# A clustered-attention, mixture-of-experts and gated feed-forward kernel: buffers of their own for the cluster sums' copy and the comparison's output

## The chip, the core and the metric

The kernel runs on one core of a Trainium2 chip. The metric is the device time of one execution in microseconds (us). The kernel before takes 869.03 us, the median of three runs that lie between 868.84 and 869.63 us.

## The reference

Three layers follow each other: attention in which a query sees only the keys of its own cluster, a layer of eight experts with one expert per token, and a gated feed-forward layer. Only the first is touched by the change. Cut to that:

```python
# q, k, v: (2, 8, 768, 64) f32; centroids: (8, 16, 64)
q_assign = argmax(einsum('bhsd,hcd->bhsc', q_n, c_n))   # nearest of 16 centroids, per head
k_assign = argmax(einsum('bhsd,hcd->bhsc', k_n, c_n))
mask   = q_assign[:, :, :, None] == k_assign[:, :, None, :]
scores = where(mask, q @ k.T / sqrt(64), -1e9)
attn   = softmax(scores)
x      = attn @ v                    # then the experts, then the gated layer
```

## The kernel before

Sixteen heads are worked through as eight pairs (`n` = 0 to 7). A pair has twelve steps `g`; in each step 128 queries of one head meet all 768 keys. TensorE makes the scores `s` (L338, two parts that are summed in PSUM: one from the tiles `Aq` and `Ak`, one from `qB` and `kB`), VectorE takes the negative row maximum `nm` (L341), ScalarE the exponential `P` (L351). TensorE turns `P` over (`t`, L367), ScalarE and VectorE copy the halves into `PT` (L370, L372), and after three steps TensorE multiplies with v (`acc`, L386). When both heads of a pair have finished a half of the queries, `onat` takes the reciprocal of the sums (`rs`, L411 and L412, VectorE), multiplies by `R` on TensorE (`on`, L416) and writes `lg` and `x` (L420, VectorE). This happens in steps 0 and 3 of the next pair.

Each engine works through its own instructions strictly in the order in which the program writes them (`manual_schedule`). Where an instruction waits, everything behind it on its engine waits too. The order inside a step is set by the list `order` in `CFG`: soft, scores, the two turns, the evacuation, one piece of preparation (B0), `onat` (O), the product with v (V0), further preparation (B1).

While pair n-1 is worked through, the next pair n is prepared in eight pieces, at the steps that `offs` gives, counted from the start of pair n-1:

- `q0` and `q1` at steps -4 and -2, `k0` and `k1` at -1 and 1 (`tr`): q and k are turned over in halves and split into a high part `Hq`, `Hk` and a low part `Lq`, `Lk` (the rounding error of the high part), and `X` is kept in full. With the second half, `moves` has SyncE issue the transfers that copy the parts into `Aq`, `Ak`, `qB`, `kB` of the pair: six for q and six for k, 192 KB each, among them `Aq<-Lq` and `kB<-Lk`, two each.
- `a` at step 2 (`assign`): the products with the centroids (`asp`), and ScalarE's copy of them into the tile `as` (L206).
- `t` at step 3 (`pick`): TensorE turns `as` over (`ast`, L213), VectorE takes the maximum per token (`mxa`, L218) and compares (`eqa`, L219), GpSimd multiplies the result by a descending count (L220).
- `f` at step 6 (`first`) picks the first maximum; `m` at step 7 (`mask`) turns the result over, ScalarE writes `oT` (L295), and SyncE issues eight small transfers `qB<-oT` and `kB<-oT` that append it to the operands of the scores.

Piece `t` stands at token B0 of step 3, and the later `onat` of the pair before follows it at token O. So VectorE's order there is `mxa`, `eqa`, `rs`, its reciprocal, `lg`, `x`.

Buffers come from pools. The pool `one` has a single buffer for each tag; two tiles with one tag share that buffer, and the writer of the second then waits for every reader of the first. In the kernel before, `as` has the tag `Lq` and `eqa` the tag `Lk`. The readers of `Lq` and `Lk` are the transfers `Aq<-Lq` and `kB<-Lk`. Pair 1 keeps its low parts in another pool (`raw`), pair 0 its own in `one`.

SyncE's queue carries, beside these moves, the loads of q, k and v of coming pairs (`load`) and eight fills of 768 KB with zeros (`moe_rows<-zero`, L594, one in every four steps from step 14 on).

Of the kernel before, what the change touches and what calls it, by code (L numbers as in the profile page):

```python
# [10 lines left out]
F32 = mybir.dt.float32  # L11
# [12 lines left out]
class Attention:  # L24
# [169 lines left out]
    def assign(self, n):  # L194

        nc, st = self.nc, self.pairs[n]
        C, HS = self.C, self.S // 2
        b, hp = divmod(n, self.H // 2)
        ps = self.ps_m.tile([128, HS], F32, tag="mm", name="asp")
        for half in range(2):  # L200
            for si, nm in enumerate("qk"):
                g = (2 * half + si) * 2 * C
                nc.tensor.matmul(ps[g:g + 2 * C], lhsT=self.cbd[:, hp, :], rhs=st["X" + nm][:, half * HS:(half + 1) * HS],
                                 start=True, stop=True, tile_position=(0, g))
        st["as"] = self.one.tile([128, HS], F32, tag="Lq", name="as")
        nc.scalar.copy(out=st["as"], in_=ps)  # L206

    def pick(self, n):
        nc, st = self.nc, self.pairs[n]
        C, HJ = self.C, self.J // 2  # L210
        ps = self.ps_m.tile([128, HJ, 128], F32, tag="mm", name="ast")
        for jj in range(HJ):
            nc.tensor.transpose(ps[:, jj, :], st["as"][:, jj * 128:(jj + 1) * 128], self.ident)  # L213
        G = HJ * 8
        psf = ps.rearrange("p j (g c) -> p (j g) c", c=C)
        mx = self.one.tile([128, G], F32, name="mxa")
        eq = self.one.tile([128, G, C], F32, tag="Lk", name="eqa")
        nc.vector.tensor_reduce(out=mx, in_=psf, axis=AX.X, op=ALU.max)  # L218
        nc.vector.tensor_tensor(out=eq, in0=psf, in1=mx.unsqueeze(2).to_broadcast([128, G, C]), op=ALU.is_equal)  # L219
        nc.gpsimd.tensor_tensor(out=eq, in0=eq, in1=self.desc.to_broadcast([128, G, C]), op=ALU.mult)  # L220
        st["eq"] = eq
# [980 lines left out]
```

## Time and profile before

| | |
|---|---|
| median of three runs | 869.03 us |
| the profiled execution's own time | 871.81 us |
| its span (first to last instruction) | 870.1 us |
| mean granted TensorE clock | 0.967 of full speed |
| attention up to pair 0's last scores | 0 to about 52 us |
| pairs 1 to 6 | about 52 to 306 us |
| pair 7 | about 306 to 342 us |
| experts and gated layer | 342 to 870 us |

The span of the profiled execution is 1.7 us shorter than its own time, and that time is 2.8 us above the median. Instructions are named by line, engine and tile, with the written tile to the left of the arrow. The clock column of the stretches is the share of full speed that TensorE was granted: 1.00 is 2.4 GHz, 0.50 is 1.2 GHz, and what lies between is a mixture of the two.

### The profile page before, as it was taken

What the parts mean: (1) busy time and instruction counts of PE and PEld (TensorE: products, weight loads), DVE (VectorE), ACT (ScalarE), POOL (GpSimd) and SP (SyncE); (2) the same over time, 40 slices, a digit from 0 to 9 for tenths busy, and PEclk for the clock granted to TensorE, in tenths of its full rate; (3) what the DMA queues carried; (4) which work ended last, traced back from release to release, by engine and by line L of the source; (5) the groups of instructions that cost most, each with busy time, mean ns of one, the idle gap of its engine ahead of it and who ended that gap; (6) DMA issues with size and microseconds to landing.
All of it is one profiled execution on the core that took longest, in us unless ns stands there. A gap on an engine that the chain in (4) does not pass through costs nothing. (4 is left out here: it accounts for less than half of the span.)

```text
span 870.1 us, 12695 instructions
## 1 busy us (share of the span) xinstructions
PE 796.2 (92%) x4791; PEld 661.3 (76%) x4791; DVE 530.9 (61%) x871; ACT 381.0 (44%) x697; POOL 191.8 (22%) x212
## 2 busy tenths in 40 slices
PE   8988787878697999899999999999999999999997
PEld 7755555556465667799999999887888888888885
DVE  5665555555556677676666565367776676676533
ACT  5664545454545565355545554245432232232110
POOL 5110101010102002640000000033433333333235
PEclk9998989798998999999999999999999999999999
DMA  9762737370705221766666666032321221220012
GB/s 199 177 146 99 174 107 176 106 168 9 165 10 139 70 86 61 266 206 206 205 194 197 200 203 194 25 97 82 112 72 52 73 71 51 73 73 0 1 49 97
DMA packets 94210, 102.04 MB, mean 117 GB/s; under 512 B 30752, under 2 KB 78752, under 8 KB 94144
## 3 DMA queue, kind: packets, MB, share of 16 engines
q1 hardware_dynamic: 89280, 89.33, 36.8%
q0 software_dynamic: 1920, 6.29, 1.9%
q10 hardware_dynamic: 2944, 5.54, 1.8%
q8 instruction: 41, 0.67, 0.3%
q14 instruction: 25, 0.20, 0.1%
HBM read 68.21 MB, written 12.58 MB: 93 GB/s over the span
## 5 line engine op out<-in xcount | busy, mean ns | idle before, releaser
L341 DVE TENSOR_REDUCE nm<-s 128x1 f32<-128x768 f32 x96 | 91.4, 952 | 77.8 <-PE s L338 77.1
L370 ACT COPY PT<-t 128x384 f32<-128x384 f32 x96 | 46.3, 482 | 129.5 <-PE t L367 128.9
L351 ACT ACTIVATE P<-s,nm 128x768 f32<-128x768 f32 x96 | 87.0, 907 | 9.2 <-DVE nm L341 5.9
L367 PE MATMUL t<-ident,P 128*128 128x128 f32 x576 | 81.5, 276 | 0.9 <-ACT PT L370 0.5
L386 PE MATMUL acc<-PT,ldv 128*64 128x384 f32 x384 | 77.1, 538 | 0.2 <-DVE rm L634 0.2
L1027 POOL TENSOR_TENSOR W1l<-cm,W1h 128x512 fp32r<-128x512 f32 x18 | 23.4, 1301 | 235.0 <-ACT W1h L1026 235.0
L367 PEld LDWEIGHTS t<-ident,P 128*128 128x128 f32 x576 | 69.1, 142 | 7.4 <-DVE PT L372 1.2
L844 PE MATMUL yp<-Hhh,W2h 128*128 128x256 f32 x256 | 73.2, 286 | 0.0
L844 PE MATMUL hp<-Xh,W1h 128*128 128x256 f32 x256 | 72.8, 284 | 0.2 <-ACT Xh L836 0.2
L844 PE MATMUL hp<-Xl,W1h 128*128 128x256 f32 x256 | 72.7, 284 | 0.3 <-DVE Xl L837 0.3
L844 PE MATMUL yp<-Hhh,W2l 128*128 128x256 f32 x256 | 72.6, 284 | 0.0
L844 PE MATMUL yp<-Hhl,W2h 128*128 128x256 f32 x256 | 72.5, 283 | 0.0
L844 PE MATMUL hp<-Xh,W1l 128*128 128x256 f32 x256 | 72.5, 283 | 0.0
L1054 POOL TENSOR_TENSOR ghl<-u,ghh 128x512 fp32r<-128x512 f32 x36 | 49.9, 1387 | 75.1 <-ACT ghh L1053 75.1
L338 PE MATMUL s<-Ak,Aq 128*128 128x384 f32 x192 | 59.5, 392 | 6.0 <-ACT P L351 6.0
L1073 DVE TENSOR_TENSOR acc<-o,acc 128x512 f32<-128x512 f32 x60 | 41.2, 691 | 31.0 <-PE o L1065 31.0
L416 PE MATMUL on<-R,O 128*128 128x144 f32 x96 | 19.9, 357 | 43.3 <-DVE rs L411 42.9
L1051 DVE TENSOR_TENSOR u<-sg,g 128x512 f32<-128x512 f32 x36 | 24.8, 688 | 54.3 <-ACT sg L1050 53.1
L338 PE MATMUL s<-kB,qB 80*128 80x384 f32 (+1 forms) x192 | 52.3, 348 | 4.8 <-DMA kB<-oT 4.0
L338 PEld LDWEIGHTS s<-Ak,Aq 128*128 128x128 f32 x192 | 29.6, 194 | 33.1 <-ACT P L351 22.8
L372 DVE COPY PT<-t 128x384 f32<-128x384 f32 x96 | 52.4, 546 | 1.5 <-PE t L367 1.5
L386 PEld LDWEIGHTS acc<-PT,ldv 128*64 128x64 f32 x384 | 27.2, 150 | 33.9 <-issue 31.8
(269 smaller groups left out, 2007.7 us busy)
## 6 DMA issues: line engine op xcount, KB each, us to landing
raw<-in_moe_w SPq DMA_DIRECT2D x64, 512.0 KB, 4.3
Ak<-Hk SPq DMA_DIRECT2D x32, 192.0 KB, 5.0
moe_rows<-zero SPq DMA_DIRECT2D x8, 768.0 KB, 6.0
raw<-in_moe_w_gate SPq DMA_DIRECT2D x12, 512.0 KB, 3.6
raw<-in_moe_w_val SPq DMA_DIRECT2D x12, 512.0 KB, 3.6
raw<-in_moe_w_out SPq DMA_DIRECT2D x12, 512.0 KB, 3.5
xr<-moe_rows ACTq DMA_DIRECT2D x7, 768.0 KB, 6.5
ldq<-in_q SPq DMA_DIRECT2D x16, 192.0 KB, 4.3
```

The costliest lines, as they stand in the source:

```text
L338: nc.tensor.matmul(ps[:, c, 0:HS], lhsT=ql[:, qs], rhs=kr[:, c * HS:(c + 1) * HS], start=a == 0, stop=a == 1)
L341: nc.vector.tensor_reduce(out=nm, in_=ps[:, :, 0:HS], axis=AX.XY, op=ALU.max, negate=True)
L351: nc.scalar.activation(out=P, in_=ps[:, :, 0:HS], func=AF.Exp, bias=nm, accum_out=self.pairs[n]["sum"][:, i, r:r + 1])
L367: nc.tensor.transpose(ps[:, jj, :], P[:, a, jj * 128:(jj + 1) * 128], self.ident)
L370: nc.scalar.copy(out=PT[:, js, cs], in_=ps)
L372: nc.vector.tensor_copy(PT[:, js, cs], ps)
L386: nc.tensor.matmul(acc[c * D:(c + 1) * D], lhsT=v[:, c * HJ + j], rhs=PT[:, c * HJ + j, :], start=j == 0, stop=j == HJ - 1, tile_position= ...
L844: self.nc.tensor.matmul(out, lhsT=W[a][:, k, cols], rhs=mov[b][:, k, :], start=i == 0, stop=i == n - 1)
L1027: nc.gpsimd.tensor_tensor(out=l, in0=m, in1=h.bitcast(F32), op=ALU.subtract)
L1051: nc.vector.tensor_tensor(out=u, in0=sg, in1=ps[0], op=ALU.mult)
L1054: nc.gpsimd.tensor_tensor(out=hl[:, fc], in0=u, in1=hh[:, fc].bitcast(F32), op=ALU.subtract)
L1073: nc.vector.tensor_tensor(out=a, in0=p[t], in1=a, op=ALU.add)
```

## The change

Two tiles lose the tag by which they shared a buffer and get one of their own name in the same pool, 1.5 KB for each of the 128 partitions apiece.

```diff
-        st["as"] = self.one.tile([128, HS], F32, tag="Lq", name="as")
+        st["as"] = self.one.tile([128, HS], F32, name="as")
...
-        eq = self.one.tile([128, G, C], F32, tag="Lk", name="eqa")
+        eq = self.one.tile([128, G, C], F32, name="eqa")
```

No instruction is added, removed or moved on any engine. What changes is the semaphores that some of them wait for. In brackets stand the semaphores: `DMAHW` with a number is a transfer of SyncE's or ScalarE's queue, `Pool`, `PE`, `DVE` and `Activation` are engines.

VectorE at step 3, in the preparation of pair 3 (difference of the two programs):

```order
 L372 COPY PT<-t 128x3x128 [waits PE_49]
 L218 TENSOR_REDUCE mxa<-ast 128x24 [waits PE_49]
-L219 TENSOR_TENSOR eqa<-ast,mxa 128x384 [waits DMAHW1_49,DMAHW6_49,DVE_49,Pool_49]
+L219 TENSOR_TENSOR eqa<-ast,mxa 128x384 [waits DVE_49]
 L411 TENSOR_SCALAR rs<-sum 128x6
 L412 RECIPROCAL rs<-rs 128x6 [waits DVE_49]
```

The comparison keeps its place between `mxa` and `rs`; its waits for two transfers and for GpSimd are gone. It is so in the preparation of pairs 2 to 7; for pair 1, whose own low parts lie in another pool, the wait that goes is one for a transfer of pair 0.

GpSimd, the comparison's multiplication and the splits of the next pair (first before, then after):

```order
-L220 TENSOR_TENSOR eqa<-eqa,desc 128x384 [waits DMAHW4_49,DMAHW1_49,DVE_49]
-L162 TENSOR_TENSOR Xq<-Hq,Lq 128x384 [waits DVE_49] x2
-L158 TENSOR_TENSOR Lk<-Xk,Hk 128x384 [waits Activation_49,Pool_49]
...
+L220 TENSOR_TENSOR eqa<-eqa,desc 128x384 [waits DVE_49,Pool_49]
+L162 TENSOR_TENSOR Xq<-Hq,Lq 128x384 [waits DVE_49] x2
+L158 TENSOR_TENSOR Lk<-Xk,Hk 128x384 [waits DMAHW1_49,DMAHW4_49,Activation_49,Pool_49]
```

The two transfers `kB<-Lk` are now waited for where the next pair's `Lk` is written, ten steps later.

ScalarE, the copy of the cluster sums and the next instructions that wait for transfers (first before, then after):

```order
-L206 COPY as<-asp 128x384 [waits DMAHW2_49,DMAHW7_49,PE_49,Pool_49]
...
-L295 ACTIVATE oT<-otp,sc 128x384 [waits DMAHW4_49,DMAHW3_49,DMAHW5_49,DMAHW1_49,DMAHW6_49,DMAHW0_49,PE_49]
-L351 ACTIVATE P,sum<-s,nm 128x768 [waits DVE_49]
-L370 COPY PT<-t 128x3x128 [waits PE_49]
-L155 ACTIVATE Hq<-trp 128x384 [waits DMAHW5_49,DMAHW1_49,DMAHW6_49,DMAHW0_49,PE_49]
...
+L206 COPY as<-asp 128x384 [waits PE_49]
...
+L295 ACTIVATE oT<-otp,sc 128x384 [waits DMAHW4_49,DMAHW3_49,DMAHW5_49,DMAHW2_49,DMAHW6_49,DMAHW1_49,DMAHW7_49,DMAHW0_49,PE_49]
+L351 ACTIVATE P,sum<-s,nm 128x768 [waits DVE_49]
+L370 COPY PT<-t 128x3x128 [waits PE_49]
+L155 ACTIVATE Hq<-trp 128x384 [waits DMAHW1_49,DMAHW5_49,DMAHW0_49,DMAHW6_49,PE_49,Pool_49]
```

The copy waits for TensorE alone; `oT` names eight transfers instead of six, all of them the eight moves of the `oT` of the pair before.

The pool is 3 KB per partition larger, so tiles that are placed behind it lie at other addresses, and in the experts' stage the first writers of a weight tile name some other transfers of the attention.

## Rows read from the trace of the kernel before

**Rows 1.** Page, part 1: busy us, share of the span and instructions of each engine.

```profile
PE 796.2 (92%) x4791; PEld 661.3 (76%) x4791; DVE 530.9 (61%) x871; ACT 381.0 (44%) x697; POOL 191.8 (22%) x212
```

**Rows 2.** Granted clock and busy time by stretch: us, engines' busy time (instructions), PEclk, DMA, GB/s.

```profile
17.00:52.30 35.30, 33.38 (x202) 25.68 (x203) 24.63 (x38) 25.11 (x55) 5.66 (x13) 0.90 0.63 147
52.30:305.90 253.60, 200.25 (x1233) 142.59 (x1232) 144.46 (x282) 130.58 (x291) 31.27 (x35) 0.91 0.47 118
305.90:342.00 36.10, 34.36 (x224) 24.31 (x223) 25.59 (x74) 21.27 (x46) 5.26 (x11) 1.00 0.15 54
```

**Rows 3.** Waits over the span: who waited <- for whom: us, times, longest us.

```profile
PE on L416 <- DVE rs L411: 42.9, 6, 8.7
...
DVE eqa L219 <- DMA kB<-Lk: 33.0, 6, 7.0
```

**Rows 4.** VectorE, preparing pair 3: start us, us, instruction [idle before <-releaser].

```profile
104.30 0.55 DVE L218 TENSOR_REDUCE mxa<-ast 128x24 f32<-128x384 f32 x1
111.12 0.56 DVE L219 TENSOR_TENSOR eqa<-ast,mxa 128x384 f32<-128x384 f32 x1 [6.27 <-DMA kB<-Lk]
...
113.64 0.21 DVE L420 TENSOR_TENSOR lg<-on,rs 128x48 f32<-128x48 f32 x1 [1.66 <-PE on L416]
...
118.20 0.96 DVE L341 TENSOR_REDUCE nm<-s 128x1 f32<-128x768 f32 x1 [3.89 <-PE s L338]
```

**Rows 5.** TensorE in order of time, the same stretch.

```profile
103.42 0.49 PE L213 MATMUL ast<-ident,as 128*128 128x128 f32 x3
111.82 1.78 PE L416 MATMUL on<-R,O 128*128 128x144 f32 x6 [7.91 <-DVE rs L411]
113.53 3.67 PE L386 MATMUL acc<-PT,ldv 128*64 128x384 f32 x12
117.12 0.62 PE L338 MATMUL s<-Ak,Aq 128*128 128x384 f32 x2
```

**Rows 6.** The stretches from each late `on` to the next `nm`; the last is undelayed.

```profile
68.50:74.36 5.86, 5.86 (x25) 3.56 (x26) 0.83 (x3) 0.00 (x0) 0.94 (x1) 0.68 0.47 181
111.82:118.20 6.38, 6.38 (x25) 3.72 (x26) 0.83 (x4) 0.00 (x0) 0.93 (x1) 0.62 0.59 207
155.43:162.20 6.77, 6.77 (x25) 3.73 (x26) 0.84 (x4) 0.00 (x0) 0.94 (x1) 0.59 0.56 197
197.38:203.64 6.26, 6.26 (x25) 3.71 (x26) 0.83 (x3) 0.00 (x0) 0.93 (x1) 0.64 0.00 0
239.73:245.30 5.57, 5.57 (x25) 3.49 (x26) 0.92 (x4) 0.00 (x0) 0.93 (x1) 0.72 0.02 4
280.28:286.07 5.79, 5.79 (x25) 3.53 (x26) 0.92 (x5) 0.00 (x0) 2.06 (x4) 0.69 0.12 45
305.87:309.86 3.99, 3.99 (x28) 2.50 (x26) 2.14 (x9) 1.54 (x5) 0.00 (x0) 1.00 0.66 221
```

**Rows 7.** ScalarE in order of time, the copy of the cluster sums.

```profile
102.14 0.51 ACT L206 COPY as<-asp 128x384 f32<-128x384 f32 x1
```

**Rows 8.** SyncE's DMA issues in order of time, pairs 3 and 4.

```profile
106.87 0.59 SPq L132 DMA_DIRECT2D kB<-Lk  x1
...
154.61 0.71 SPq L594 DMA_DIRECT2D moe_rows<-zero  x1
171.18 1.23 SPq L132 DMA_DIRECT2D qB<-oT  x2
```

**Rows 9.** Two-us stretches: a short TensorE wait, a long one, pair 4's last transfers.

```profile
88.00:90.00 2.00, 0.69 (x3) 0.37 (x3) 0.00 (x0) 0.00 (x0) 0.00 (x0) 1.00 0.11 26
...
106.00:108.00 2.00, 0.00 (x0) 0.00 (x0) 0.00 (x0) 0.00 (x0) 0.00 (x0) 0.59 0.97 243
...
158.00:160.00 2.00, 2.00 (x10) 0.79 (x8) 0.00 (x0) 0.00 (x0) 0.00 (x0) 0.50 0.57 219
```

**Rows 10.** DMA issues from 60 to 140 us: count, KB each, median us to landing.

```profile
kB<-Lk SPq DMA_DIRECT2D x4, 192.0 KB, 4.8
...
kB<-oT SPq DMA_DIRECT2D x8, 24.0 KB, 1.9
```

## The prediction

> **What bounds the kernel now.** I read the page's first part, then the busy time by stretch, then the list of waits, then VectorE and TensorE in order of time around the longest wait. TensorE is busy for 92% of the span [rows 1], so the kernel looks bound by matmuls. That share is a mean over unlike stages. By stretches, pair 0 takes 35.3 us and pair 7 takes 36.1 us with TensorE busy for 95% of each, but the six pairs between take 253.6 us, 42.3 us each, with TensorE busy for 79% and its clock at 0.91 [rows 2]. These six pairs are where time is lost.
>
> The list of waits names the place. VectorE's comparison `eqa` waits for the transfer `kB<-Lk` six times, 33.0 us in total, and TensorE's `on` waits for VectorE's `rs` six times, 42.9 us in total [rows 3]. In order of time it is one event. While pair 3 is prepared, `mxa` starts at 104.30 and `eqa` at 111.12 after 6.27 us of idleness [rows 4]. `rs` stands behind `eqa`, and `on` stands on TensorE ahead of everything else, so TensorE ends `ast` at 103.91 and does nothing for 7.91 us [rows 5]. The transfer was issued at 106.87 [rows 8], at the end of a long burst of moves and loads on SyncE's queue.
>
> The second loss follows the first. TensorE's clock is 1.00 before the wait; in the stretch 106 to 108 the mean is 0.59 [rows 9], and when work resumes it still runs at the low level of 1.2 GHz: `on` takes 1.78 us, the product `acc` 3.67 us [rows 5], and the stretch from the start of `on` to the next `nm` has a clock of 0.59 to 0.72 in all six pairs [rows 6].
>
> **The change part by part.**
>
> The comparison. Nothing reads its new buffer but its own chain, so its waits for transfers go, and `eqa` starts as soon as `mxa` ends. I take away just the idleness that the trace charges to the transfer: 33.0 us, six times [rows 3]. `on` starts 0.70 us after `eqa` (111.12 to 111.82) in the trace [rows 4, 5], with no other wait between, so it moves by the same amount. TensorE keeps a gap here: 7.91 less 6.27, so 1.64 us, in which `mxa`, `eqa` and `rs` run.
>
> The clock. From the start of `on` to the next `nm` the six late pairs take 5.86, 6.38, 6.77, 6.26, 5.57 and 5.79 us, together 36.63. The same instructions at full clock, in pair 7, take 3.99 us [rows 6]; six of these are 23.94. The difference is 12.7 us. Whether it comes back depends on whether 1.64 us of idleness leaves the clock alone. The nearest row says so: TensorE was busy for only 0.69 of the 2 us from 88 to 90, 1.31 us idle, with the clock at 1.00 [rows 9]. So I take 12.7; the other end of this term is 0. The page "TensorE: Matmul & The Clock Gate" of the Trainium skill (section on oscillation in real kernels) describes a loop that stops for a transfer again and again and starts each piece at the low clock. Read as a rule for every repeated stop, it would keep the stretches of rows 6 as they are and give the result of rival 2; the row with the short wait speaks against that reading here.
>
> The sums' copy. ScalarE starts `as` at 102.14 with no idle time before it [rows 7]: its transfers were issued steps earlier. Its wait goes for nothing, and it costs nothing.
>
> Waits that are added. On GpSimd the next pair's `Lk` now waits for the two transfers that `eqa` used to await. They land about 4.3 us after 106.87, so at 111.1, and that `Lk` is written ten steps on, some 29 us later by 35 us to a pair. VectorE's `Lq` likewise names moves of a pair earlier. On ScalarE `oT` and `Hq` name transfers that the old copy had taken note of for them; those are moves of the pair before. If one of these were late, ScalarE's exponentials and copies would queue behind `oT`, and TensorE behind them. All were issued more than half a pair earlier, so I put this at nothing; the upper bound is rival 4.
>
> What is late next. The scores of the next pair, from step 10, need the eight mask moves that SyncE issues at step 7, and now that point comes earlier while the burst's transfers keep their place up to the removed wait. Pair 4 is the tightest: its mask moves start at 171.18 [rows 8]; less 7.0 us of wait [rows 3] and 2.8 us of clock (6.77 less 3.99) [rows 6] that is 161.4. The burst's last issue is at 154.61 [rows 8], and the DMA engines are busy for 0.57 of the stretch 158 to 160 [rows 9], so the tail is over by about 159.2. Some 2 us remain, and the moves find empty queues as now. Cost nothing; the other end is rival 3. The page "DMA: Bandwidth & Descriptors" of the Trainium skill (section on queues, rings and completion order) says that each DMA engine takes its descriptors in ring order, so a small move behind a burst would have to wait its turn; by that rule the order would cost something only if the 2 us were gone.
>
> The experts' stage. The larger pool shifts addresses, and the first writers of weights name some other transfers of the attention, all long past. Nothing.
>
> **The sum.** 33.0 + 12.7 = 45.7 us. The profiled execution takes 871.81 us, 2.78 us above the median of the runs shown; it would take 826.1, and the median of 869.03 becomes 823.3 us. A cross-check that uses neither term: six pairs in 253.6 less 45.7 are 207.9 us, 34.7 each, beside 35.3 for pair 0, which prepares a pair without such a wait, and 36.1 for pair 7 [rows 2]. So the forecast asks of the six pairs only what pair 0 already does; were they to match 35.3 exactly, the gain would be 253.6 - 211.8 = 41.8 us and the time 827.2.
>
> **The rivals.**
>
> 1. The change does not do what it says: the comparison then waits for something else, and the time stays at 869. For it: a wait for several semaphores is put down to the last one only, and the old instruction also waited for GpSimd. Against it: GpSimd's `Lk` must be finished before the transfer that reads it can be issued, and the remaining wait is for VectorE's own `mxa`.
>
> 2. The wait goes, but the clock stays low around step 3, because a gap of 1.64 us remains six times. Then 869.0 - 33.0 = 836.0 us. Against it: the 1.31 us wait that left the clock at 1.00 [rows 9].
>
> 3. The mask moves meet the tail of the burst. A move inside a burst (`kB<-Lk`) takes a median of 4.8 us to land, a mask move on empty queues 1.9 us [rows 10]. If all six pairs lost the difference of 2.9 us at the next scores, 17.4 us are given back: 840.7 us. For it: only 2 us are spare in pair 4. Against it: pairs 5 to 7 issue no zero fills and their bursts end earlier, and the wait of rows 9 sits behind SyncE's issue time, not behind traffic.
>
> 4. Slower. The stop reappears at step 7 to 10: `oT` or the first scores wait for moves that are queued behind the burst, with TensorE stopped long enough for its clock to fall again. What is saved is 45.7 / 6 = 7.6 us a pair, so this turns to slower only if the new stop is over 7.6 us a pair. At 9 us, as long as today's longest stop of TensorE, 8.7 us [rows 3], it would be 823.3 + 54 = 877 us. Against it: the burst starts when `Hq` is ready, which moves with the compute, so its tail cannot slide so far past step 7.
>
> **How the numbers follow.** The forecast, 823 us, has 0.77; its own range is 819 to 829, from the cross-check and a few us of small shifts. Rival 2 has 0.09, rival 3 has 0.07, rival 1 has 0.02 and rival 4 has 0.02; 0.03 is left for a gain beyond 50 us, since TensorE's gap before `on` might close further. The range 817 to 837 takes in rival 2 and the forecast, 0.86 in all, less something for misjudged sizes inside them. Differences under 0.2%, 1.7 us, can't be told from no change here. Faster: 0.77 + 0.09 + 0.07 + 0.03 = 0.96. The same: 0.02. Slower: 0.02.
>
> **What the profile of the changed kernel would show.** The row of `eqa` waiting for `kB<-Lk` is gone from the list of waits, and `on` waits for `rs` about 1.6 us at a time, near 10 us in total. From the start of `on` to the next `nm` the six stretches take about 4.0 us at a clock of 1.00. The six pairs take about 208 us. The stretches before 52 us and after pair 7 keep their length. The wait of the scores for `kB<-oT` stays near 1.3 us; if it grows to 4 us, rival 3 is at work, and if the six stretches stay near 6 us with the waits gone, rival 2. The prediction is wrong if another wait of several us appears at `eqa`, `oT` or the scores of step 10.

## The result and the profile after

The changed kernel takes 829.77 us, the median of four runs between 826.61 and 831.73; the kernel before, now over four runs, 869.33. The ratio is 0.954 with a 95% interval of 0.950 to 0.957. The forecast was 823.3 us with a range of 817 to 837: the sign, the place and the mechanism were right, the gain is 39.6 us where 45.7 were forecast.

The profiled execution took 829.75 us with a span of 827.7 us. First the list of waits (who waited, for whom, us in total, times, longest), beside [rows 3]:

```profile
PE on L416 <- DVE rs L411: 10.1, 6, 1.7
...
PE s L338 <- DMA kB<-oT: 4.8, 6, 1.8
```

The row of `eqa` waiting for `kB<-Lk`, 33.0 us before, is not there any more, and `on` waits 10.1 us instead of 42.9. What is left of it is six times 1.68 us, in which VectorE works off `mxa`, `eqa` and `rs`. In the preparation of pair 3 VectorE shows it in order of time, beside [rows 4]:

```profile
96.76 0.55 DVE L218 TENSOR_REDUCE mxa<-ast 128x24 f32<-128x384 f32 x1
97.34 0.56 DVE L219 TENSOR_TENSOR eqa<-ast,mxa 128x384 f32<-128x384 f32 x1
...
99.06 0.21 DVE L420 TENSOR_TENSOR lg<-on,rs 128x48 f32<-128x48 f32 x1 [0.85 <-PE on L416]
...
102.12 0.96 DVE L341 TENSOR_REDUCE nm<-s 128x1 f32<-128x768 f32 x1 [2.39 <-PE s L338]
```

`eqa` follows `mxa` at once. TensorE in the same stretch, beside [rows 5]:

```profile
95.88 0.49 PE L213 MATMUL ast<-ident,as 128*128 128x128 f32 x3
98.05 0.97 PE L416 MATMUL on<-R,O 128*128 128x144 f32 x6 [1.68 <-DVE rs L411]
98.95 2.16 PE L386 MATMUL acc<-PT,ldv 128*64 128x384 f32 x12
```

The gap is 1.68 us instead of 7.91, `on` takes 0.97 us instead of 1.78, and the product 2.16 instead of 3.67. The six stretches from the start of `on` to the next `nm` (length first; third number from the end is the granted clock), beside [rows 6]:

```profile
62.28:66.34 4.06, 4.06 (x25) 2.56 (x26) 0.83 (x3) 0.00 (x0) 0.99 (x1) 1.00 1.00 276
98.05:102.12 4.07, 4.07 (x25) 2.58 (x26) 0.82 (x3) 0.00 (x0) 0.99 (x1) 1.00 0.98 242
132.38:136.44 4.06, 4.06 (x25) 2.57 (x26) 0.83 (x4) 0.00 (x0) 1.00 (x1) 1.00 1.00 228
166.69:170.77 4.08, 4.08 (x25) 2.59 (x26) 0.84 (x4) 0.00 (x0) 0.99 (x1) 1.00 0.73 198
203.32:207.38 4.06, 4.06 (x25) 2.57 (x26) 0.91 (x4) 0.00 (x0) 0.99 (x1) 1.00 0.68 178
238.01:242.08 4.07, 4.07 (x25) 2.57 (x26) 0.92 (x4) 0.43 (x2) 2.12 (x4) 1.00 0.97 295
```

All six are at full clock, 24.4 us together where they were 36.6. By stretches (pair 0; pairs 1 to 6; pair 7; the 43 us behind it), beside [rows 2]:

```profile
17.00:51.60 34.60, 32.11 (x202) 24.59 (x203) 24.39 (x38) 24.94 (x55) 5.62 (x12) 0.95 0.64 149
51.60:261.90 210.30, 189.33 (x1232) 137.83 (x1231) 144.69 (x282) 130.66 (x291) 31.19 (x35) 0.99 0.55 142
261.90:298.00 36.10, 34.35 (x224) 24.29 (x223) 25.63 (x74) 21.21 (x46) 5.24 (x10) 1.00 0.15 54
298.00:341.00 43.00, 39.79 (x292) 37.46 (x291) 27.96 (x69) 19.32 (x26) 27.72 (x29) 0.96 0.60 200
```

The six pairs fell from 253.6 to 210.3 us, by 43.3. Two clocks below 1.00 are left, and the reader should note them: 0.99 in the six pairs, although the six stretches above are at 1.00, and 0.96 behind attention, where the kernel before had 1.00.

### The profile page after: what moved, and what is told of

It is laid out like the page before. It is cut to its first block, busy times and chain, and to the rows that moved or that the text cites. A ratio compares the mean times of both kernels' runs of the same rounds, so it can differ in the third digit from the quotient of the medians.

```text
span 827.7 us, 12686 instructions
## 1 busy us (share of the span) xinstructions
PE 785.4 (95%) x4791; PEld 656.6 (79%) x4791; DVE 531.2 (64%) x871; ACT 380.8 (46%) x697; POOL 191.9 (23%) x212
## 5 line engine op out<-in xcount | busy, mean ns | idle before, releaser
L386 PE MATMUL acc<-PT,ldv 128*64 128x384 f32 x384 | 69.7, 495 | 0.2 <-DVE rm L634 0.2
L338 PEld LDWEIGHTS s<-Ak,Aq 128*128 128x128 f32 x192 | 29.3, 192 | 32.8 <-ACT P L351 23.1
L1053 ACT CAST ghh<-u 128x512 fp32r<-128x512 f32 x36 | 22.4, 622 | 67.9 <-DVE u L1052 67.9
L844 PEld LDWEIGHTS hp<-Xl,W1h 128*128 128x128 f32 x256 | 49.9, 195 | 0.5 <-DVE Xl L837 0.5
```

The costliest lines, as they stand in the source:

```text
L338: nc.tensor.matmul(ps[:, c, 0:HS], lhsT=ql[:, qs], rhs=kr[:, c * HS:(c + 1) * HS], start=a == 0, stop=a == 1)
L386: nc.tensor.matmul(acc[c * D:(c + 1) * D], lhsT=v[:, c * HJ + j], rhs=PT[:, c * HJ + j, :], start=j == 0, stop=j == HJ - 1, tile_position= ...
L844: self.nc.tensor.matmul(out, lhsT=W[a][:, k, cols], rhs=mov[b][:, k, :], start=i == 0, stop=i == n - 1)
```

## The experiments

Theory: the whole gain is the comparison's wait for the transfer `kB<-Lk`, together with the low clock that follows it. The rivals were that the copy `as` has a part in it, that the wait was really for GpSimd, and that TensorE is slow after the wait for another reason than its clock. In the first group the kernel before took 871.35 us in the same session (13 runs, 868.48 to 873.22).

**Only the copy in its own buffer.**

```diff
-        st["as"] = self.one.tile([128, HS], F32, tag="Lq", name="as")
+        st["as"] = self.one.tile([128, HS], F32, name="as")
```

> Of the kernel before, with only the copy of the cluster sums (as) in a buffer of its own; the comparison still shares the buffer of Lk. Theory (the whole gain is the comparison's wait for kB<-Lk and the low clock behind it): 869 us, within 0.3%, and eqa still waits about 33 us in six waits. Rival (the copy's wait takes part, by holding ScalarE): 829.8 + something under 39, a measurable gain of at least 2 us.

Measured: 870.6 us, ratio 0.999 (0.998 to 1.001).

```profile
DVE eqa L219 <- DMA kB<-Lk: 31.9, 6, 7.5
```

The wait is all there. This half of the change is worth nothing that can be measured.

**Only the comparison in its own buffer.**

```diff
-        eq = self.one.tile([128, G, C], F32, tag="Lk", name="eqa")
+        eq = self.one.tile([128, G, C], F32, name="eqa")
```

> Of the kernel before, with only the comparison's output (eqa) in a buffer of its own; as still shares the buffer of Lq. Theory: the time of the changed kernel, 829.8 us within its spread of 826.6 to 831.7, no wait of eqa. Rival (as, now the first to take note of the moves of Lq, holds ScalarE once the comparison no longer does): some us above 832, with as waiting for Aq<-Lq in the list of waits.

Measured: 827.33 us (824.39 to 827.84), ratio 0.948 (0.945 to 0.952). The interval overlaps that of the whole change, and no wait of `eqa` or `as` is listed. One line of the two makes the gain. Pairs 1 to 6 and the stretch behind attention in its profile:

```profile
52.30:261.40 209.10, 188.00 (x1232) 136.19 (x1231) 144.45 (x282) 130.70 (x290) 31.24 (x35) 1.00 0.56 143
...
297.50:341.00 43.50, 40.38 (x310) 38.03 (x309) 28.67 (x70) 20.59 (x28) 28.52 (x30) 1.00 0.64 213
```

Here both clocks are 1.00, though the comparison's wait is gone here too. The two falls of the clock in the profile of the whole change thus do not follow from the removal of that wait by itself.

**Shared buffers as before, but the loads of q and k behind the moves of `Lk`.**

```diff
-CFG = {..., 'load': 0}
+CFG = {..., 'load': 4}
```

> The kernel before with both buffers shared as before; the loads of q and k of the next pair are issued four steps later, so that they stand behind the moves of Lk on SyncE's queue. Theory (the comparison waits for the landing of the last kB<-Lk, which the burst delays): the moves are issued up to 4 us sooner, bounded by the time at which Lk is written, the six waits fall from 33 us to 10 to 20 us, and the time to 838 to 856 us, the lower end if the clock no longer falls. Rival (the comparison really waits for GpSimd's write of Lk, and the transfer is only named last): nothing changes on GpSimd, 33 us and 869 us.

Measured: 863.82 us, ratio 0.990 (0.987 to 0.994). The waits fell from 33.0 to 23.8 us, not to the 10 to 20 that were expected, and the time by 7.5 us, not to the 838 to 856 that were expected. First GpSimd's write of `Lk`, then SyncE's issues, then VectorE's comparison, while pair 3 is prepared:

```profile
101.44 1.01 POOL L158 TENSOR_TENSOR Lk<-Xk,Hk 128x384 fp32r<-128x384 f32 x1 [5.30 <-ACT Xk L157]
```

```profile
104.38 0.76 SPq L132 DMA_DIRECT2D kB<-Lk  x1
105.18 0.95 SPq L594 DMA_DIRECT2D moe_rows<-zero  x1
106.17 2.71 SPq L120 DMA_DIRECT2D ldq<-in_q  x2
```

```profile
104.64 0.55 DVE L218 TENSOR_REDUCE mxa<-ast 128x24 f32<-128x384 f32 x1
108.92 0.56 DVE L219 TENSOR_TENSOR eqa<-ast,mxa 128x384 f32<-128x384 f32 x1 [3.73 <-DMA kB<-Lk]
```

`Lk` is finished at 102.45. The last move of it is issued 0.26 us before `mxa` starts, where before it was 2.57 us after [rows 4, 8], and the wait is 2.54 us shorter: 3.73 us instead of 6.27. `eqa` starts at 108.92, 4.5 us after the issue. GpSimd was done 6 us before `eqa` started, so the wait was for the transfer: it follows the issue of the transfer and not the end of `Lk`. My size was wrong since most of the wait, 23.8 of 33.0 us, does not come from the loads ahead in the queue. The moves of `k` go out as two of `Hk`, one of `Lk`, two of `Hk` and one of `Lk`, so the last `Lk` still stands behind all the others, and it takes its time to land even so.

**Shared buffers and the wait as before, with idle turns of the identity on TensorE.**

```diff
             nc.tensor.transpose(ps[:, jj, :], st["as"][:, jj * 128:(jj + 1) * 128], self.ident)
+        if n > 1:
+            self.warm(self.ps_t, "t", 44)
```

> The kernel before with both buffers shared and its wait in place; TensorE turns the identity matrix 44 times (about 5.4 us) into a scratch PSUM tile between ast and on, in the preparation of pairs 2 to 7. Theory (12.7 us of the gain are TensorE at the low clock after the idle time): eqa still waits about 33 us, the six stretches from on to the next nm fall from 5.6 to 6.8 us to about 4.0 us at full clock, and the time to 869.3 - 12.7 = 856.6 us, 855 to 860. Rival (on and acc are slow after the wait for another reason, such as the burst of transfers that is still under way): the stretches keep their length and the time is 869 us or above.

Measured: 859.82 us, ratio 0.987 (0.983 to 0.990), a gain of 11.5 us (8 to 15 by the interval) while `eqa` still waits 32.7 us in six waits. The six stretches from the start of `on` to the next `nm`, beside [rows 6]:

```profile
65.25:69.32 4.07, 4.07 (x25) 2.57 (x26) 0.83 (x4) 0.00 (x0) 0.93 (x1) 1.00 0.82 306
107.31:112.96 5.65, 5.65 (x25) 3.52 (x26) 0.83 (x4) 0.00 (x0) 0.92 (x1) 0.71 0.41 158
150.23:155.94 5.71, 5.71 (x25) 2.97 (x26) 0.83 (x3) 0.00 (x0) 0.93 (x1) 0.70 0.57 209
191.10:195.17 4.07, 4.07 (x25) 2.57 (x26) 0.83 (x3) 0.00 (x0) 0.93 (x1) 1.00 0.00 0
230.00:234.07 4.07, 4.07 (x25) 2.58 (x26) 0.92 (x5) 0.00 (x0) 0.93 (x1) 1.00 0.01 2
268.71:272.77 4.06, 4.06 (x25) 2.57 (x26) 0.91 (x4) 0.00 (x0) 2.06 (x4) 1.00 0.18 69
```

The turns ended before the wait did in all six, by 0.15 to 4.28 us. In the two with the longest rest, 4.28 and 3.60 us, the clock fell after all; in the second stretch `on` took 1.78 us (line numbers are two higher in this kernel):

```profile
98.01 5.03 PE L429 MATMUL warm<-ident 128*128 128x128 f32 x44
107.31 1.78 PE L418 MATMUL on<-R,O 128*128 128x144 f32 x6 [4.28 <-DVE rs L413]
```

So the clock term stands by itself: in four of six pairs the stretch fell to 4.07 us with the wait still in place, in the first of them with the DMA engines still busy for 0.82 of it. But not all of the 11.5 us is this term. The six stretches take 27.6 us instead of 36.6, which is 9.0; another 1.9 us of the profiled execution are shorter waits for `kB<-oT` (2.1 us instead of 4.0), which I had not forecast and whose reason no run shows. That the time fell into the expected range is in part luck.

The second group started from the changed kernel and looked for what the forecast missed; the kernel before took 870.63 us in it (7 runs).

**`onat` and the product with v ahead of the first piece of preparation.**

```diff
-CFG = {..., 'order': ['S', 'Q', 'T0', 'T1', 'E', 'B0', 'O', 'V0', 'B1'], ...}
+CFG = {..., 'order': ['S', 'Q', 'T0', 'T1', 'E', 'O', 'V0', 'B0', 'B1'], ...}
```

> The changed kernel with another order inside a step: onat and the product with v come before the first piece of preparation (list order: O, V0, B0 in place of B0, O, V0). Theory (after the change TensorE still loses about 1.7 us six times, 10.1 us in all, because on stands behind eqa's rs): on waits for rs 0 to 0.4 us at a time and the time falls by 6 to 10 us against the changed kernel, to 0.940 to 0.943 of the kernel before. Rival (the gap only moves: ast then waits for on's PSUM buffer, first and mask come later, and the scores at step 10 wait longer for kB<-oT): 0.948 to 0.954, as the changed kernel, with the wait for kB<-oT over 2 us each.

Measured: 818.85 us, ratio 0.940 (0.936 to 0.944), against 0.954 of the change alone: 10.9 us less than the changed kernel, a little more than the 6 to 10 expected. `on` has no wait for `rs` in the list any more. VectorE now waits for `ast` (10.5 us in seven waits), and TensorE has the product with v to do in that time.

```profile
DVE mxa L218 <- PE ast L213: 10.5, 7, 1.7
...
PE s L338 <- DMA kB<-oT: 4.4, 6, 1.5
```

**`first` and `mask` one step earlier.**

```diff
-CFG = {..., 'offs': [..., ['f', 6], ['m', 7]], ...}
+CFG = {..., 'offs': [..., ['f', 5], ['m', 6]], ...}
```

> The changed kernel with first and mask one step earlier (5 and 6 in place of 6 and 7). Theory (what the forecast missed inside the six pairs is the wait of the scores for kB<-oT, 11.5 us in the two lists of matmuls and weight loads together, about 1.6 us a pair, with a fall of the clock behind it in one pair): that wait goes, the clock stays at 1.00 in all six pairs, and the time falls by 8 to 12 us against the changed kernel, to 0.937 to 0.943 of the kernel before. Rival (the moves then meet the tail of the burst, which in pairs 2 to 4 ends only some us earlier): half of it or less, 0.944 to 0.954, with the wait left in those pairs.

Measured: 822.28 us, ratio 0.944 (0.941 to 0.948), just above the expected range and at the lower end of the rival's; but the rival's sign, a wait that is left, is not there. The wait for `kB<-oT` is gone and the clock of the six pairs is 1.00, but a shorter wait takes its place, since `mask` turns over what `first` has only just written:

```profile
PE otp L294 <- DVE oh L231: 2.4, 6, 0.5
```

The pairs take 204.6 us, 5.7 less than in the changed kernel, and not the 8 to 12 I had added up. I had summed the wait of the matmuls (4.8 us) and that of the weight loads (6.7 us), which overlap: they are the same stop, seen on two rows.

**Both.** The edits are the two above.

> The changed kernel with both edits, the order of the step and first and mask one step earlier. Theory: the two gains lie at different steps and add: 14 to 20 us under the changed kernel, 0.927 to 0.936 of the kernel before, pairs 1 to 6 together 190 to 196 us. Rival (one of the gaps was cover for the other, or VectorE becomes the bound): no better than the better of the two alone.

Measured: 810.89 us, ratio 0.931 (0.928 to 0.934). Pairs 1 to 6 take 192.6 us. The gains add.

**Both, and 33 in place of 26 idle matmuls behind attention.**

```diff
-        for i in range(26):
+        for i in range(33):
```

> As the kernel with both edits, and 33 instead of 26 idle matmuls between attention and the experts, 1.7 us more, which fill the wait for xr. Theory (the 1.6 us that the changed kernel's profile lost behind attention are the first expert at the low clock after that wait): clock 1.00 in the stretch behind attention, and within 1 us of the kernel with both edits, on the lower side. Rival (the wait for xr is longer than the matmuls or they delay it): 1 to 3 us above it.

Measured: 810.61 us, ratio 0.931 (0.928 to 0.934); the four runs lie between 810.22 and 810.78. The stretch behind attention, without and with the seven more:

```profile
281.00:324.00 43.00, 39.94 (x294) 37.60 (x292) 28.14 (x68) 19.32 (x26) 27.89 (x30) 0.96 0.60 203
```

```profile
280.30:323.00 42.70, 41.20 (x310) 38.60 (x309) 28.23 (x69) 20.26 (x27) 28.49 (x30) 1.00 0.63 213
```

The clock stays up, but the difference of 0.3 us in the median is inside what can be measured. That the falls of the clock make the spread of the changed kernel (5 us) fits with this kernel's 0.6 us, and with the changed kernel's slowest run (831.73 us) having the lowest mean clock, 0.989, and its fastest (826.61 us) the highest, 0.995; four runs of each do not prove it. This and the kernel with both edits are the fastest versions found, 60 us under the kernel before.

## Why the prediction was right, and where its size was off

**The comparison.** Right. The wait went as a whole and nothing took its place at `eqa`; TensorE's wait for `rs` fell by 32.8 us where 33.0 were forecast, and its remaining gap is 1.68 us where 1.64 were forecast. That this buffer alone does it, and that the copy's wait costs nothing that can be measured, the first two experiments show.

**The clock at step 3.** Right in size: 36.6 to 24.4 us is 12.2, forecast 12.7; the missing half microsecond is nearly all `on`, at 0.97 us instead of 0.90 six times. The gap of 1.68 us left the clock at 1.00 all six times, so rival 2 did not come about, and the fourth experiment shows the term apart from the wait.

**What is late next.** Put at nothing; a small loss came, and not in the pair that the forecast watched. The wait of TensorE's scores for `kB<-oT` grew from 4.0 to 4.8 us over six pairs. Before:

```profile
PE s L338 <- DMA kB<-oT: 4.0, 6, 1.3
```

Pair 4 lost nothing. Its mask moves started at 145.42, 7.8 us behind the last issue of the burst, the DMA engines stood idle from 143 to 145, and its scores waited 0.34 us as before. The waits that grew are those of the scores of pair 2 (1.33 to 1.80 us) and of pair 5 (1.32 to 1.60 us). It is not rival 3 there either: the DMA engines stood idle in 72 to 74 and in 176 to 178, just before these two sets of mask moves. But the slowest `kB<-oT` of the two sets took 3.3 and 3.1 us to land (2.8 and 2.9 before) where those of pairs 3 and 4 took at most 2.0; the median of 1.9 us [rows 10] does not show that, and why it is so stays open. Behind the wait of pair 5's scores, which are first worked on in step 10 of pair 4, the clock fell:

```profile
186.69 0.44 PE L338 MATMUL s<-kB,qB 80*128 80x384 f32 x1 [1.60 <-DMA kB<-oT]
...
187.98 0.99 PE L338 MATMUL s<-Ak,Aq 128*128 128x384 f32 x2
```

```profile
188.00:190.00 2.00, 2.00 (x9) 1.90 (x8) 1.94 (x6) 1.85 (x4) 0.16 (x1) 0.50 0.00 0
```

From one step-0 `on` to the next pair 4 takes 36.63 us; in the kernel with only the comparison's buffer, where the clock held, 35.48. That is 1.15 us, of which 0.15 is a longer wait (1.60 us against 1.45). With the 0.8 us of longer waits and the half microsecond of `on` this makes up nearly all of the 2.4 us by which the six pairs missed the 207.9 us forecast.

**The experts' stage.** Put at nothing; in the profiled execution it took 1.6 us more, from the last `on` to the end of the span (530.5 before, 532.0 after). The first expert began behind a wait for `xr` of 1.78 us, which ended at 311.91. Its first matmuls still ran at full clock, and some 2 us later the clock fell:

```profile
308.00:312.00 4.00, 2.22 (x11) 1.52 (x10) 1.33 (x11) 0.00 (x0) 3.74 (x3) 1.00 0.67 212
312.00:316.00 4.00, 3.42 (x19) 2.98 (x20) 1.29 (x2) 1.47 (x3) 4.00 (x4) 0.76 0.95 300
```

It does not follow from the shifted addresses: the kernel with only the comparison's buffer waited 1.69 us there with a clock of 1.00 and took 530.6 us, as before, and the kernel with `first` and `mask` one step earlier, whose pool is as large as that of the changed kernel, waited 1.68 us, also with a clock of 1.00.

**The sum.** In the profiled executions: 43.3 us in the six pairs, 0.7 in pair 0, less 1.6 behind attention, is 42.4 us of span. That is 3.3 less than the 45.7 forecast. (Pair 0's 0.7 us are not the change's: its clock was 0.95 instead of 0.90, and the profiles of the other kernels show either.) The step that was mis-sized most after that is the last one, the way from the profiled execution to the median. I took 45.7 us from 869.03, the median of three runs, though the durations came from an execution of 871.81 us. Later sessions put the kernel before at 871.35 and 870.63 us, so the three runs were on the low side, and about 2 us of the miss are of that kind. The cross-check with pair 0, 827.2 us, was nearer to the result than the sum, but that is in part luck. Pair 0's 35.3 us hold a loss of their own, a clock of 0.90 [rows 2], which the six pairs no longer have, and the 34.7 us that were set beside it came from the sum itself.

**The rivals.** Rival 1 fell with the third experiment as well as with the result: the wait followed the transfer, with GpSimd done 6 us earlier. Rivals 2, 3 and 4 did not come about.

## What to carry to other kernels

A wait for a transfer at an instruction that does not use the transferred data can be the sign of a shared buffer, as it was here; look at which tiles share a tag, and at who reads the earlier one. Price such a stop on the engine that is stopped in the end, and add what TensorE's clock loses behind it: here 12 us beside 33. Once the large stop is gone, the short ones are worth the same look: two reorderings of the program took another 19 us.

## What was not expected of the hardware

The length of a short wait does not tell whether TensorE's clock falls behind it. In the profile of the changed kernel TensorE idled 1.68 us six times before `on` and 1.80 us before the scores of pair 2, and the clock was 1.00 in the 4 us behind each:

```profile
82.47 0.44 PE L338 MATMUL s<-kB,qB 80*128 80x384 f32 x1 [1.80 <-DMA kB<-oT]
```

```profile
82.47:86.47 4.00, 3.66 (x26) 3.37 (x27) 3.46 (x6) 2.93 (x7) 0.85 (x1) 1.00 0.13 30
```

Yet 1.60 us before the scores of pair 5 and 1.78 us before the first expert were followed by a fall, about 1 and 2 us after work had resumed. Before the first expert the other kernels show the same: the clock fell behind 1.62 us (the order of the step) and 1.63 us (both edits), and held behind 1.68 us (`first` and `mask` earlier) and 1.69 us (only the comparison's buffer). What else TensorE did before these waits differs, and no run here separates that. The forecast took one row, 1.31 us of idleness with the clock at 1.00, as a sign that a gap of 1.64 us would leave the clock alone. It did so six times of six at `on`, but as a rule for short waits it does not hold.
